# Batch 2's u centred by ScalarE, and the order around it: a fused attention, Fourier and two-layer kernel on one core

## The chip, the core and the metric

The kernel runs on one core of one Trainium2 chip. A core has five engines that run side by side, each through its own queue in order: TensorE (PE) for matmuls, VectorE (DVE), ScalarE (ACT) and GpSimd (POOL) for elementwise work, and SyncE (SP), which here issues nearly all DMAs. PE writes its results to PSUM; everything else is in SBUF or in DRAM. The metric is the time of one execution on the device in microseconds; the median of four runs before is 304.16 us (303.73 to 304.6).

## What is computed

Two blocks follow one another. Attention between x (8 batches, 8 heads, 512 rows, 64 columns) and a state of 32 rows gives 544 rows of 512 columns for each batch. The second block takes the real part of a two-dimensional Fourier transform of these rows, adds it, normalises and runs two layers with a residual.

```python
scores = scale * np.matmul(x, state.transpose(0, 1, 3, 2))      # softmax over the state rows
xread = np.matmul(softmax(scores), state)
scores2 = scale * np.matmul(state, x.transpose(0, 1, 3, 2))     # softmax over x's rows
sread = np.matmul(softmax(scores2), x)
x = np.concatenate([xread, sread], axis=2)                      # then (8, 544, 512)
mixed = np.real(np.fft.fft(np.fft.fft(x, axis=1), axis=2))
u = x + mixed
un = (u - mean(u)) / np.sqrt(var(u) + 1e-06)
out = u + np.maximum(un @ w_ch1, 0.0) @ w_ch2                   # 512 -> 2048 -> 512
```

The kernel computes the Exp of the scores without subtracting their maximum, and divides after the product. The division by the standard deviation (`rstd`) is put off to the very end, since it is positive and passes through the Relu: the layers work on u minus its mean, and the store multiplies by `rstd` and adds u.

## The kernel before

All engines run in the order in which the program text issues their instructions[...]. So the order of the calls is the schedule, and each call adds its instructions to the queues of several engines at once. A wait of the first instruction in a queue holds everything behind it.

A batch goes through these stages; the names are those of the code.

- `load_x`, `cast_x` bring x from DRAM as seven DMAs of SP, and POOL casts it to bf16 (`xin`).
- `attend(b)` gives two lists of steps. The first holds the scores: the transposes of x and state (`xT`, `sT`: by PE for batches 0 and 1, by SP's DMA transposes from batch 2 on, called `turned[b]`), then `scores` (x by state, Exp by ACT to `E`). The attention of x needs Exp of the scores the other way round, `ET`. Batch 1 computes it with matmuls of its own (`scores_t`, Exp again); from batch 2 on `turn_scores` turns `E` by matmuls with `ident` and `mirror`, and ACT's copy to `ET` also yields the sums over the rows. The second list R holds the reads: `read_low`, POOL's `fold_low` steps, `read(0)`, `sread_heads` or `sread_by_head`, `read(128)`, and `read(256)` with the folds. Each `xread` takes the one PSUM tile of pool psX, which DVE frees with its multiplication (L466).
- The folds add and subtract mirrored rows and columns (L529 to L549 on DVE, L514 to L526 on POOL), so that the Fourier matrices are a quarter of their size.
- `transform(b)` gives the steps T: four `over_s` (transform over rows, `G`), two `over_d` (over columns, `yp`), `add` (u, DVE), `centre` (statistics by DVE, u minus its mean to `ub`), `turn_u` (the transpose of `ub` to `unT`: by PE for batches 0 and 1, by a DMA transpose of SP (L852) from batch 2 on), `done`. u has four tiles of 128 rows, (0,1), (0,0), (1,1), (1,0) in this order. `flipped` names the batches whose `ub` ACT makes, with the sign turned.
- `layer1(b)` has 16 steps of four matmuls (0.86 us of PE each), each followed by a Relu of ACT to `hT`. For batch 0 they are quarter steps of sixteen small matmuls. A step takes a PSUM tile of pool psF, which has three.
- `layer2(b)` has 16 steps, four for a tile of u; the last of four stores: DVE multiplies and adds (L962, `ot`), SP issues the DMA. Of the first and the last tile the rows go through `r_dram`; the way back out of `r_dram` is issued just before the next store.

`first_roots` holds the computation of `rstd` (two POOL instructions, L343 and L344) for batches 0 and 1, which are called later than their statistics (`spread` for batch 0).

The opening (batches 0 and 1) is an order written out by hand. There L is `layer1(0)`, M is `layer2(0)`, s1 and r1 are the lists of `attend(1)`. Then a loop runs over b from 1 to 8. Pass 1 is by hand as well: M1 is what is left of `layer2(0)` (M1[0] is M[7]), L1 is `layer1(1)`, R and T belong to batch 2, s3 to batch 3. From pass 2 on `weave` merges the streams by position: each stream has a start and an end between 0 and 1, and its steps are spread evenly between. In pass 2 six steps of `layer2(1)` stand in the first 0.22, `layer1(2)` starts at 0.18, batch 3's reads run from 0.08 to 0.43, its T steps from 0.55 to 0.88. Worked out, pass 2 begins M M M R0 M R1 M R2 M and then the first step of `layer1(2)`, which needs all four tiles of `unT` of batch 2.

Three POOL copies to `gate` exist only to make POOL wait: for x's landing before the second half of w2 is loaded (L1162), for batch 1's folds before batch 2's x is cast (L1176), and for the last part of w2 before the last columns of it are cast (L1180). SP's transposes of x for batch 2 (`turned[2]`) wait for that last cast, and in SP's queue behind them stand `load_x(3)`, batch 0's first two stores, `turned[3]`, the state of the later batches, `load_x(4)`, the third store, and then the transposes of batch 2's `ub` with the fourth store after the first of them.

Of the kernel before, what the change touches and what calls it, by code (L numbers as in the profile page):

```python
# [15 lines left out]
AF = mybir.ActivationFunctionType  # L16
# [14 lines left out]
def kernel(  # L31
# [8 lines left out]
    nc = tc.nc  # L40
# [288 lines left out]
    def qt(name, dt=F32):  # L329
        return psQ.tile([128, 512 if dt == F32 else 1024], dt, name=name, tag="q")  # L330
# [29 lines left out]
    def attend(b):  # L360
# [52 lines left out]
        copies = []  # L413


        def scores_t(g):
            p = qt("eTp")
            for cols, rows in ((slice(0, 128), slice(0, 128)), (slice(128, 256), slice(255, 127, -1)),
                               (slice(256, 416), slice(256, 416)), (slice(416, 512), slice(511, 415, -1))):
                for hp in range(2):  # L420
                    nc.tensor.matmul(p[:, cols], lhsT=sT[:, 2 * g + hp, :], rhs=xT[:, 2 * g + hp, rows],
                                     start=(hp == 0), stop=(hp == 1))
            nc.scalar.activation(ET[:, g, :], p, AF.Exp, scale=scale)


        def scores(i):
            p = qt("esp")
            for si in (2 * i, 2 * i + 1):
                for pr in range(4):
                    hp = pr % 2  # L430
                    o = (si % 2) * 256 + pr * 64
                    nc.tensor.matmul(  # L432
                        p[:, o:o + 64].rearrange("p (h j) -> p h j", j=Ns),
                        lhsT=xT[:, pr, si * 128:(si + 1) * 128],
                        rhs=sT[:, pr, 64 * hp:64 * hp + 64].rearrange("p (h j) -> p h j", j=Ns)[:, :, ::-1 if b < 2 else 1],
                        start=True, stop=True)
            nc.scalar.activation(E[:, 2 * i:2 * i + 2].rearrange("p a b c -> p (a b c)"), p, AF.Exp, scale=scale)

# [48 lines left out]
        def sread_heads():  # L487
            p = qt("srp")
            for g in range(2):
                for si in range(4):  # L490
                    for hh in range(4):
                        c0 = 1 + 256 * g + 64 * hh
                        nc.tensor.matmul(p[32 * hh:32 * hh + 32, 64 * g:64 * g + 64], lhsT=E[:, si, g, 32 * hh:32 * hh + 32],
                                         rhs=xin[:, si, c0:c0 + 64], start=(si == 0), stop=(si == 3))
            for g in range(2):
                for si in range(4):
                    nc.tensor.matmul(p[:, 128 + g:129 + g], lhsT=E[:, si, g, :], rhs=xin[:, si, 0:1], start=(si == 0), stop=(si == 3))
            rcs = wk.tile([128, 2], F32, name="rcs", tag="rcs")
            nc.vector.reciprocal(rcs, p[:, 128:130])
            nc.vector.tensor_tensor(XQ[:, 0:2 * D].rearrange("p (g d) -> p g d", g=2),  # L500
                                    in0=p[:, 0:128].rearrange("p (g d) -> p g d", g=2),
                                    in1=rcs.unsqueeze(2).to_broadcast([128, 2, D]), op=ALU.mult)

        def state_rows():
            p = qt("hdp")
            pv = p[0:32, :].rearrange("p (h g d) -> p h g d", h=4, g=2)
            for hh in range(4):
                nc.tensor.matmul(pv[:, hh], lhsT=ident[:, 32 * hh:32 * hh + 32], rhs=XQ[:, 0:2 * D].rearrange("p (g d) -> p g d", g=2),
                                 start=True, stop=True)
            nc.scalar.copy(XR[0:32, 0, 512:0:-1].rearrange("p (g h d) -> p h g d", g=2, d=D), pv)  # L510

# [44 lines left out]
        if b < 2:  # L556
            first = [turn_state, lambda: turn_x(0), lambda: turn_x(1)]
            if b == 1:
                first = [turn_all] + [lambda i=i: copies[i]() for i in range(3)]
            first += [lambda: scores_t(0), lambda: scores_t(1),  # L560
                     lambda: scores(0), lambda: scores(1)]
        else:
            first = [lambda: scores(0), lambda: scores(1), lambda: turn_scores(1), lambda: turn_scores(0)]
            if b >= x_by_dma:
                turned[b] = lambda: (b > 2 and turn_state(), turn_x(0), turn_x(1))
                turned[b, 0] = turn_state
            else:
                first = [turn_state, lambda: turn_x(0), lambda: turn_x(1)] + first
# [129 lines left out]


    un_of, tiles_of = {}, {}  # L700
    flipped = (0, 1)

    def transform(b):
        g4, bq = b // 4, b % 4
# [154 lines left out]
        def done():  # L859
            tiles = []  # L860
            for k, r in order:
                if True:
                    u = U[k][:, r, 0:512] if r == 0 else U[k][:, r, 512:0:-1]
                    dst = {(0, 0): out[b, 1:129, :], (1, 1): out[b, 273:401, :], (0, 1): (b, 0, 543), (1, 0): (b, 1, 271)}[k, r]
                    tiles.append((u, rstds[k, r], dst))
            tiles_of[b] = tiles
            if b:
                keep_middle()
# [24 lines left out]
    def low_rows(g4):  # L893
# [15 lines left out]
        def turn_u():  # L909
            nc.sync.dma_start_transpose(out=unT, in_=m["ub"])  # L910
            dst = g4
            tiles_of[key] = [(m["U"], m["rstd"], dst)]

        return [over_d, centre, turn_u]

# [36 lines left out]
    def layer2(key):  # L952
# [2 lines left out]
        po_of = {}  # L955

        def store(i, cols):
            u, rstd, dst = tiles_of[key][i]
            while later:
                later.pop()()  # L960
            ot = wk.tile([128, dm], F32, name="ot", tag="ot", bufs=4)
# [168 lines left out]
    keep_low()  # L1130
    clears(1)
    clear_state(2, 3)
    state_blocks(2, 3, nc.gpsimd.tensor_copy)
    make_mirror()
    clear_state(3, 4)
    nc.gpsimd.tensor_tensor(gate, xs_of[0][:, 0:4], w1[:, :, 3 * 512], op=ALU.add)
    second_weights(0, 2)
# [2 lines left out]
    turned[2, 0]()  # L1140
    load_state(3, 4, s_dram)
    turn_u(0, 1)
    add_sums(0, 0)
    centre_sums(0, 0)
    copies1[0]()
    copies1[1]()
    warm(4)
    L[0]()
    s1[0]()
    copies1[2]()  # L1150
    L[1]()
    turn_u(0, 0)
    s1[1]()
    add_sums(1, 1)
    centre_sums(1, 1)
    add_sums(1, 0)
    L[2]()
    s1[2]()
    r1[0]()
    r1[1]()  # L1160
    r1[2]()
    nc.gpsimd.tensor_copy(gate, xs_of[2].rearrange("p (i c) -> p i c", i=4)[:, :, 0])  # L1162
    second_weights(2, 4)
    clear_state(4, B)
    L[3]()
    s1[3]()
    r1[3]()
    centre_sums(1, 0)
    L[4]()
    r1[4]()  # L1170
    r1[5]()
    turn_u(1, 1)
    L[5]()
    r1[6]()
    r1[7]()
    nc.gpsimd.tensor_copy(gate, XQs[1].rearrange("p (g j c) -> p g j c", g=2, j=4)[:, 1, 3, 0:4])  # L1176
# [5 lines left out]
    turned[2]()  # L1182
    load_x(3)
    turn_in_dram(4, B)
    L[6]()
    L[7]()
    turn_u(1, 0, nc.scalar.copy)
    spread(0, 1)
    state_ones(2, B)
    L[8]()  # L1190
    L[9]()
    L[10]()
    L[11]()
    over_s1(0)
    over_s1(1)
    L[12]()
    over_s1(2)
    over_s1(3)
    keep_middle()
    L[13]()  # L1200
    over_d1(0)
    add1(0, 1)
    L[14]()
    centre1(0, 1)
    over_d1(1)
    add1(0, 0)
    L[15]()
    centre1(0, 0)
    add1(1, 1)
    M[0]()  # L1210
    turn_u1(0, 1, nc.scalar.copy)
    M[4]()
    centre1(1, 1)
    add1(1, 0)
    M[1]()
    turn_u1(0, 0, nc.scalar.copy)
    centre1(1, 0)
    M[5]()
    M[2]()
    turn_u1(1, 1)  # L1220
# [74 lines left out]
```

## Time and profile before

| What | Value |
|---|---|
| median of four runs | 304.16 us |
| the profiled execution | 304.57 us |
| its span, first to last instruction | 302.8 us |
| DVE busy | 178.7 us (59%) |
| ACT busy | 136.6 us (45%) |
| POOL busy | 91.8 us (30%) |
| a step of layer 1 or 2 (four matmuls of 512 columns), start to start | 0.86 us |
| Relu of a step (ACT, L933) | 597 ns |
| `ub` by DVE (L847) / by ACT for batch 1 (L845) | 514 / 722 ns |
| statistics of a tile (DVE, L337 and L339) | 682 + 182 ns |
| `ot` of a store (DVE, L962) | 747 ns |
| `rstd` of a tile (POOL, L343 and L344) | 191 + 590 ns |

The page of a profile shows one execution: the busy time of each engine, the span in 40 slices (digits are tenths), the clock granted to PE, the chain of work that ended last, and groups of instructions by line. A line such as L962 is a line of the kernel. Besides the page the trace answers in time order (a timeline: start, length, engine, line, and in brackets how long the engine stood and who released it) and by stretches of time. The difference of 1.8 us between the profiled execution's time and its span lies before the first and after the last instruction.

### The profile page before, as it was taken

What the parts mean: (1) busy time and instruction counts of PE and PEld (TensorE: products, weight loads), DVE (VectorE), ACT (ScalarE), POOL (GpSimd) and SP (SyncE); (2) the same over time, 40 slices, a digit from 0 to 9 for tenths busy, and PEclk for the clock granted to TensorE, in tenths of its full rate; (3) what the DMA queues carried; (4) which work ended last, traced back from release to release, by engine and by line L of the source; (5) the groups of instructions that cost most, each with busy time, mean ns of one, the idle gap of its engine ahead of it and who ended that gap; (6) DMA issues with size and microseconds to landing.
All of it is one profiled execution on the core that took longest, in us unless ns stands there. A gap on an engine that the chain in (4) does not pass through costs nothing.

```text
span 302.8 us, 6030 instructions
## 1 busy us (share of the span) xinstructions
PE 288.0 (95%) x2302; PEld 164.9 (54%) x2333; DVE 178.7 (59%) x445; ACT 136.6 (45%) x254; POOL 91.8 (30%) x227
## 2 busy tenths in 40 slices
PE   5999998989969999999999999999999999999995
PEld 4789984545524545466544554455444544555443
DVE  8867987275938397664838485766668474000012
ACT  6888684535503553246533535244523442334200
POOL 6765944450391033500424022602240131000000
PEclk9999999999979999999999999999999999999999
DMA  8998993956863744566353784254333133500354
GB/s 155 193 204 184 169 148 70 190 114 141 172 142 79 164 114 71 122 140 157 48 129 73 158 154 89 71 122 87 81 80 69 37 85 82 130 6 29 95 129 125
DMA packets 110824, 34.86 MB, mean 115 GB/s; under 512 B 101980, under 2 KB 106332, under 8 KB 110796
## 3 DMA queue, kind: packets, MB, share of 16 engines
q1 hardware_dynamic: 100076, 28.72, 44.1%
q0 software_dynamic: 4224, 4.19, 9.5%
q10 hardware_dynamic: 6496, 1.57, 2.5%
q8 instruction: 18, 0.29, 0.4%
q14 instruction: 10, 0.08, 0.1%
HBM read 22.41 MB, written 14.02 MB: 120 GB/s over the span
## 4 chain that ended last, share of the span: by engine, by line
PE 85%; DVE 8%; issue 2%; ACT 2%; POOL 1%; DMA 1%; DVEq 0%; POOLq 0%
PE po L995 35%; PE ph L931 32%; PE ph L941 5%; PE gp L788 3%; PE yp L684 1%; PE yp L685 1%; PE po L987 1%; DVE ot L962 1%; PE xrp L457 1%; PE xfp L457 1%; PE esp L432 1%; DVE U L689 1%; DVE st L337 1%; PE eTp L444 1%; DMA unT<-ub 1%
## 5 line engine op out<-in xcount | busy, mean ns | idle before, releaser
L995 PE MATMUL po<-w,hT 128*128 128x512 bf16 x480 | 121.2, 379 | 2.2 <-ACT hT L933 0.9
L933 ACT ACTIVATE hT<-ph 128x512 bf16<-128x512 f32 x112 | 66.9, 597 | 123.9 <-PE ph L931 120.6
L931 PE MATMUL ph<-unT,w 128*128 128x512 bf16 x433 | 112.9, 381 | 3.4 <-DMA unT<-ub 2.4
L931 PEld LDWEIGHTS <-w 128*128 128x128 bf16 x576 | 50.6, 98 | 50.5 <-issue 4.5
L995 PEld LDWEIGHTS <-hT 128*128 128x128 bf16 x496 | 46.7, 98 | 47.8 <-issue 1.0
L962 DVE SCALAR_TENSOR_TENSOR ot<-po,rstd,U 128x512 f32<-128x512 f32 (+2 forms) x33 | 24.1, 731 | 50.6 <-PE po L995 48.4
L792 POOL COPY GL<-G 128x128 bf16<-128x128 bf16 x7 | 2.0, 291 | 73.9 <-ACT G L789 73.9
L337 DVE BATCH_NORM_STATS2 st<-U 128x6 f32<-128x512 f32 x32 | 21.8, 682 | 0.1
L689 DVE TENSOR_TENSOR U<-yp,XR 128x512 f32<-128x512 f32 x14 | 9.5, 682 | 20.1 <-PE yp L685 20.1
L344 POOL TENSOR_TENSOR rstd<-rstd,mhalf 128x1 f32<-128x1 f32 x34 | 20.1, 590 | 2.7
L343 POOL TENSOR_TENSOR rstd<-mv,epst 128x1 f32<-128x1 f32 x34 | 6.5, 191 | 45.3 <-DVE mv L339 45.3
L941 PE MATMUL ph<-unT,w 128*128 128x128 bf16 x256 | 16.2, 219 | 0.3 <-DVE unT L857 0.3
L941 PEld LDWEIGHTS <-w 128*128 128x128 bf16 x256 | 15.0, 98 | 0.5 <-issue 0.4
L789 ACT CAST G<-gp 128x288 bf16<-128x288 f32 x28 | 12.8, 483 | 4.4 <-PE gp L788 4.4
L847 DVE TENSOR_SCALAR ub<-U,mv 128x512 bf16<-128x512 f32 x24 | 12.3, 514 | 0.9
L148 POOL CAST xin<-xs 128x2048 bf16<-128x2048 f32 (+1 forms) x9 | 11.7, 1319 | 3.6 <-PE xfp L457 3.5
L943 ACT ACTIVATE hT<-ph 128x512 bf16<-128x512 f32 x16 | 9.5, 594 | 4.8 <-PE ph L941 4.7
L484 DVE TENSOR_TENSOR XR<-srp,rcs 32x128 bf16<-32x128 f32 x24 | 6.9, 287 | 6.4 <-PE srp L477 5.3
L514 POOL COPY XT<-XR 32x514 bf16<-32x514 bf16 x7 | 4.3, 608 | 19.9 <-DVE XR L466 19.9
L466 DVE TENSOR_TENSOR XR<-xrp,rs 128x512 bf16<-128x512 f32 x14 | 9.7, 695 | 0.5
L466 DVE TENSOR_TENSOR XF<-xfp,rs 128x512 bf16<-128x512 f32 x14 | 9.7, 692 | 0.5
L689 DVE TENSOR_TENSOR U<-yp,XF 128x510 f32<-128x510 f32 x14 | 9.4, 673 | 0.0
(245 smaller groups left out, 373.3 us busy)
## 6 DMA issues: line engine op xcount, KB each, us to landing
xs<-in_x_dram SPq DMA_DIRECT2D x22, 256.0 KB, 4.8
w<-in_moe_w_ch_dram POOLq DMA_DIRECT2D x8, 512.0 KB, 9.9
out_dram<-ot SPq DMA_DIRECT2D x15, 256.0 KB, 3.5
r_dram<-ot SPq DMA_DIRECT2D x14, 256.0 KB, 2.2
out_dram<-r_dram SPq DMA_DIRECT2D x14, 256.0 KB, 3.5
xs<-in_x_dram SPq DMA_DIRECT2D x8, 192.0 KB, 4.6
xs<-in_x_dram ACTq DMA_DIRECT2D x2, 256.0 KB
l_dram<-ot SPq DMA_DIRECT2D x2, 256.0 KB
```

Source lines behind the costliest of these rows:

```text
L148: copy(xin_bufs[b % 2][:, lo:hi, 1:513], xs_of[b].rearrange("p (i c) -> p i c", i=4)[:, lo:hi])
L337: nc.vector.bn_stats(st6, u)
L344: nc.gpsimd.tensor_tensor(rstd, rstd, mhalf, op=ALU.pow)
L466: nc.vector.tensor_tensor(ov, in0=p[ps, :, 0:256].rearrange("p g (h d) -> p g h d", d=D), in1=rs[ps].unsqueeze(3).to_broadcast([n, 2, 4, D ...
L689: nc.vector.tensor_add(u.rearrange("p (k r) -> p k r", r=2), p.rearrange("p (r k) -> p k r", r=2)[:, 0:u.shape[1] // 2, :], x.rearrange("p ...
L789: nc.scalar.copy(G[:, j, :].rearrange("p (i q) -> p q i", q=2), p[:, 0:NM].rearrange("p (q i) -> p q i", q=2))
L847: nc.vector.tensor_scalar(t, in0=ud, scalar1=mv[:, 0:1], scalar2=None, op0=ALU.subtract)
L931: nc.tensor.matmul(ph[:, o:o + n], lhsT=w1[:, c, f * 128:(f + 1) * 128], rhs=un_of[key][:, c, :], start=(c == 0), stop=(c == DC - 1))
L933: nc.scalar.activation(hT[:, per * i:per * i + per, :].rearrange("p a b -> p (a b)"), ph, AF.Relu, scale=-1.0 / 512 if key == 0 else -1.0 ...
L941: nc.tensor.matmul(ph[:, o:o + 128], lhsT=w1[:, c, f * 128:(f + 1) * 128], rhs=un_of[key][:, c, 128 * r:128 * r + 128], start=(c == 0), st ...
L962: nc.vector.scalar_tensor_tensor(ot[:, cols], in0=po_of[i][:, 0:cols.stop - cols.start], scalar=rstd, in1=u[:, cols], op0=ALU.mult, op1=AL ...
L995: nc.tensor.matmul(po_of[i], lhsT=h_of[key][:, f, i * 128:(i + 1) * 128], rhs=w2[:, f, :], start=(f == 0), stop=(f == FC - 1))
```

## The change

- Batch 1 loses `scores_t`. It now uses `scores` and `turn_scores` as the later batches do; its state is no longer taken in reverse order in `scores`, so `sread_heads` takes its sums from `turn_scores` and its rows are turned by `mirror` in `state_rows`. `make_mirror` goes ahead of `state_blocks(2, 3)` on POOL, the three copies of batch 1's transposes go ahead of `add_sums(0, 0)`, and the steps L and M stand two places further on against the reads and the T steps.
- `flipped` holds batch 2 too: ACT makes its four `ub`, and layer 1's Relu takes them with the sign turned.
- Of batch 0's statistics, `spread(1, 1)` and `spread(1, 0)` go behind the second store, with all roots but two. So that `done` can be called before, a tile holds a function that looks its `rstd` up.
- In pass 1, L1 starts later, `sread_by_head` (R[3]) goes ahead of `read(0)` (R[2]), the third store (M1[4]) goes between `read(0)` and `read(128)`, and M1[5], M1[6], M1[7] go further ahead of L1.
- In pass 2 seven steps of `layer2(1)` stand in the first 0.25, `layer1(2)` starts at 0.22, the reads at 0.1, the T steps at 0.57. Worked out: M M M R0 M R1 M M R2 M R3 and then `layer1(2)`; the load of x for batch 5 comes behind the store of batch 1's second tile, not ahead of it.

```diff
-        def scores_t(g):
-            p = qt("eTp")
...
-                    nc.tensor.matmul(p[:, cols], lhsT=sT[:, 2 * g + hp, :], rhs=xT[:, 2 * g + hp, rows],
-                                     start=(hp == 0), stop=(hp == 1))
-            nc.scalar.activation(ET[:, g, :], p, AF.Exp, scale=scale)
...
-                        rhs=sT[:, pr, 64 * hp:64 * hp + 64].rearrange("p (h j) -> p h j", j=Ns)[:, :, ::-1 if b < 2 else 1],
+                        rhs=sT[:, pr, 64 * hp:64 * hp + 64].rearrange("p (h j) -> p h j", j=Ns),
...
-            for g in range(2):
-                for si in range(4):
-                    nc.tensor.matmul(p[:, 128 + g:129 + g], lhsT=E[:, si, g, :], rhs=xin[:, si, 0:1], start=(si == 0), stop=(si == 3))
-            nc.vector.reciprocal(rcs, p[:, 128:130])
+            nc.vector.reciprocal(rcs, sums)
...
-                nc.tensor.matmul(pv[:, hh], lhsT=ident[:, 32 * hh:32 * hh + 32], rhs=XQ[:, 0:2 * D].rearrange("p (g d) -> p g d", g=2),
+                nc.tensor.matmul(pv[:, hh], lhsT=mirror[:, 96 - 32 * hh:128 - 32 * hh], rhs=XQ[:, 0:2 * D].rearrange("p (g d) -> p g d", g=2),
...
-            first += [lambda: scores_t(0), lambda: scores_t(1),
-                     lambda: scores(0), lambda: scores(1)]
+            first += [lambda: scores(0), lambda: scores(1), lambda: turn_scores(1), lambda: turn_scores(0)]
...
-    flipped = (0, 1)
+    flipped = (0, 1, 2)
...
-                    tiles.append((u, rstds[k, r], dst))
+                    tiles.append((u, lambda k=k, r=r: rstds[k, r], dst))
...
-            u, rstd, dst = tiles_of[key][i]
+            u, root, dst = tiles_of[key][i]
+            rstd = root()
...
+    make_mirror()
     state_blocks(2, 3, nc.gpsimd.tensor_copy)
-    make_mirror()
...
+    copies1[0]()
+    copies1[1]()
+    copies1[2]()
     add_sums(0, 0)
     centre_sums(0, 0)
-    copies1[0]()
-    copies1[1]()
     warm(4)
     L[0]()
     s1[0]()
-    copies1[2]()
+    s1[1]()
     L[1]()
     turn_u(0, 0)
-    s1[1]()
     add_sums(1, 1)
-    centre_sums(1, 1)
     add_sums(1, 0)
     L[2]()
     s1[2]()
+    s1[3]()
+    centre_sums(1, 1)
+    L[3]()
+    L[4]()
     r1[0]()
     r1[1]()
     r1[2]()
...
-    L[3]()
-    s1[3]()
+    L[5]()
+    r1[4]()
     r1[3]()
     centre_sums(1, 0)
-    L[4]()
-    r1[4]()
+    turn_u(1, 1)
+    L[6]()
     r1[5]()
-    turn_u(1, 1)
-    L[5]()
+    L[7]()
     r1[6]()
     r1[7]()
...
     turn_u1(1, 1)
-    M[6]()
+    done()
+    first_roots[0]()
+    M[3]()
+    spread(0, 0)
     turn_u1(1, 0)
-    spread(0, 0)
-    spread(1, 1)
-    spread(1, 0)
-    done()
-    for root in first_roots[0:1] + first_roots[5:8] + first_roots[1:5]:
-        root()
-    M[3]()
+    first_roots[5]()
     done1()
...
-        early, until, start = {2: (6, 0.22, 0.18), 3: (3, 0.13, 0.1)}.get(b, (0, 0, 0.08))
+        early, until, start = {2: (7, 0.25, 0.22), 3: (3, 0.13, 0.1)}.get(b, (0, 0, 0.08))
...
+            def spreads():
+                spread(1, 1)
+                spread(1, 0)
+                for root in first_roots[6:8] + first_roots[1:5]:
+                    root()
+
-            for step in (M1[0], L1[0], M1[1], s2[0], s2[1], M1[2], L1[1], s2[2], s2[3], lambda: cast_x(3), turned[3], M1[3], L1[2],
-                         lambda: load_state(4, B, s_dram), lambda: load_x(4), R[0], L1[3], R[1], R[2], L1[4], M1[4], R[3], L1[5], R[4],
-                         L1[6], R[6], L1[7], L1[8], M1[5], R[7], L1[9], M1[6], R[8], L1[10], L1[11], T[0], T[1], L1[12], T[2], T[3],
-                         M1[7], T[4], L1[13], T[5], s3[0], L1[14], T[6], s3[1], L1[15], T[7], M1[8], T[8], s3[2], s3[3], T[9], T[10],
+            for step in (M1[0], spreads, M1[1], M1[2], s2[0], s2[1], L1[0], M1[3], s2[2], s2[3], L1[1], lambda: cast_x(3), turned[3], L1[2],
+                         lambda: load_state(4, B, s_dram), lambda: load_x(4), R[0], L1[3], R[1], R[3], L1[4], R[2], L1[5], M1[4], R[4],
+                         L1[6], M1[5], R[6], L1[7], R[7], L1[8], M1[6], R[8], L1[9], L1[10], M1[7], T[0], T[1], L1[11], T[2], T[3],
+                         L1[12], T[4], L1[13], T[5], s3[0], L1[14], T[6], s3[1], L1[15], T[7], M1[8], T[8], s3[2], s3[3], T[9], T[10],
...
-            reads, mix = {2: ((0.08, 0.43), (0.55, 0.88)), 3: ((0.03, 0.4), (0.5, 0.86))}.get(b, ((0, 0.375), (0.47, 0.85)))
+            reads, mix = {2: ((0.1, 0.45), (0.57, 0.88)), 3: ((0.03, 0.4), (0.5, 0.86))}.get(b, ((0, 0.375), (0.47, 0.85)))
```

Between `turn_u(1, 0, nc.scalar.copy)` of batch 0 and `turn_u1(1, 1)`, which the diff above leaves out, the `over_s1`, `over_d1`, `add1`, `centre1` and `turn_u1` calls keep their order, and the L and M steps between them are those two places further on. Three steps of PE's work still stand between `over_d1(0)` and `turn_u1(0, 1)`; from `turn_u1(0, 0)` on it is one step fewer than before.

More of the change, by code (lines that the diff above doesn't have):

```diff
@@ L413, in attend @@
         copies = []
-        def scores_t(g):
-            p = qt("eTp")
-            for cols, rows in ((slice(0, 128), slice(0, 128)), (slice(128, 256), slice(255, 127, -1)),
-                               (slice(256, 416), slice(256, 416)), (slice(416, 512), slice(511, 415, -1))):
-                for hp in range(2):
-                    nc.tensor.matmul(p[:, cols], lhsT=sT[:, 2 * g + hp, :], rhs=xT[:, 2 * g + hp, rows],
-                                     start=(hp == 0), stop=(hp == 1))
-            nc.scalar.activation(ET[:, g, :], p, AF.Exp, scale=scale)
         def scores(i):
@@ L911, in turn_u @@
             dst = g4
-            tiles_of[key] = [(m["U"], m["rstd"], dst)]
+            tiles_of[key] = [(m["U"], lambda: m["rstd"], dst)]
         return [over_d, centre, turn_u]
@@ L1184 @@
     turn_in_dram(4, B)
-    L[6]()
-    L[7]()
+    L[8]()
+    L[9]()
     turn_u(1, 0, nc.scalar.copy)
@@ L1189 @@
     state_ones(2, B)
-    L[8]()
-    L[9]()
     L[10]()
     L[11]()
+    L[12]()
+    L[13]()
     over_s1(0)
     over_s1(1)
-    L[12]()
+    L[14]()
     over_s1(2)
@@ L1199 @@
     keep_middle()
-    L[13]()
+    L[15]()
     over_d1(0)
     add1(0, 1)
-    L[14]()
+    M[0]()
     centre1(0, 1)
@@ L1206 @@
     add1(0, 0)
-    L[15]()
+    M[4]()
     centre1(0, 0)
     add1(1, 1)
-    M[0]()
+    M[1]()
     turn_u1(0, 1, nc.scalar.copy)
-    M[4]()
     centre1(1, 1)
+    M[5]()
     add1(1, 0)
-    M[1]()
     turn_u1(0, 0, nc.scalar.copy)
     centre1(1, 0)
-    M[5]()
     M[2]()
+    M[6]()
     turn_u1(1, 1)
-    M[6]()
+    done()
+    first_roots[0]()
+    M[3]()
+    spread(0, 0)
     turn_u1(1, 0)
-    spread(0, 0)
-    spread(1, 1)
-    spread(1, 0)
-    done()
-    for root in first_roots[0:1] + first_roots[5:8] + first_roots[1:5]:
-        root()
-    M[3]()
+    first_roots[5]()
     done1()
```

## The prediction

> **What bounds the kernel now.** I read the page first: TensorE (PE) is busy 95% of a span of 302.8 us, and the chain that ended last is 85% PE. So a change can gain only where PE stands still, runs at a lower clock, or has work taken away. The page's row of PE clock shows one dent.
>
> ```profile
> PE   5999998989969999999999999999999999999995
> PEclk9999999999979999999999999999999999999999
> ```
>
> The busy time by stretches of about 3 us around the dent, and then the lines of PE's own timeline that end a wait (in brackets: its length and what ended it), give its size.
>
> ```profile
> 85.00:87.80 2.80, 0.44 (x3) 0.02 (x1) 0.69 (x2) 0.00 (x0) 2.62 (x6) 0.93 0.42 94
> 87.80:90.90 3.10, 2.96 (x38) 1.31 (x40) 0.55 (x2) 0.60 (x1) 3.10 (x6) 0.51 0.90 190
> ```
>
> ```profile
> 52.47 1.02 PE L995 MATMUL po<-w,hT 128*128 128x512 bf16 x4 [0.90 <-ACT hT L933]
> 64.53 0.40 PE L457 MATMUL xrp<-stb,ET 128*128 128x260 bf16 x2 [0.86 <-DVE XF L466]
> 84.19 0.40 PE L457 MATMUL xfp<-stb,ET 128*128 128x260 bf16 x2 [0.56 <-DVE XR L466]
> 87.81 1.87 PE L931 MATMUL ph<-unT,w 128*128 128x512 bf16 x4 [2.37 <-DMA unT<-ub]
> ```
>
> In the first fence PE's busy time is the figure after the length, the clock the third from the end. PE stands 2.37 us until the last transposed quarter of batch 2's u has landed; then the clock is 0.51 for some 3 us, and four matmuls take 1.87 us instead of 1.03. From 87.81 to 90.9 half the speed is lost: about 1.5 us. The three other waits are the largest before it.
>
> Who is late with unT? The critical chain blames VectorE (DVE). SyncE's (SP) timeline tells more:
>
> ```profile
> 47.00 5.12 SPq L388 DMA_TRANSPOSE xT<-xin  x4
> 52.17 5.36 SPq L145 DMA_DIRECT2D xs<-in_x_dram  x7
> 57.57 0.62 SPq L155 DMA_DIRECT2D s_dram<-in_state_dram  x1
> ...
> 78.38 0.38 SPq L966 DMA_DIRECT2D out_dram<-ot  x1
> 78.96 1.24 SPq L852 DMA_TRANSPOSE unT<-ub  x1
> 81.95 0.35 SPq L976 DMA_DIRECT2D r_dram<-ot  x1
> 82.76 3.83 SPq L852 DMA_TRANSPOSE unT<-ub  x3
> ```
>
> From 47.00 to 80.20 SP issues nearly without a break (one pause of 2.5 us for r_dram to land, at 59). The first transpose of u leaves at 78.96 though its ub was ready at 77.15. Then SP stands from 80.20 to 81.95 at the store of batch 0's last tile, which waits for DVE:
>
> ```profile
> 80.75 0.52 DVE L847 TENSOR_SCALAR ub<-U,mv 128x512 bf16<-128x512 f32 x1
> 81.19 0.73 DVE L962 SCALAR_TENSOR_TENSOR ot<-po,rstd,U 128x512 f32<-128x512 f32 x1
> ```
>
> Three transposes of about 1.25 us queue behind that store. So two queues in series, DVE and SP, set the dent.
>
> [...]waits of 0.9 us at 52 and 64 cost no clock.[...]
>
> **Opening (22 to 43 us).** Removed: `scores_t`, twice 0.45 us of PE (23.31 to 23.76, 24.88 to 25.32), and eight sum matmuls, 0.22 (29.59 to 29.81). Added: `turn_scores` twice, by batch 2's row 0.24 each. Net PE -0.63. On ACT two Exp of 0.60 become two Copy of 0.59 with a 0.2 accumulator read. What it gives back: add_sums(0,0) stands behind a DVE copy of 0.6 us and holds its PSUM tile until about 23.8, so the second Scores step may wait 0.3; read(128) and read(256) share one PSUM tile and now stand only one 0.89 step apart, with a DVE centring and copy (0.9) between: 0.5 together; the folds end about 1 us later, just when over_s1(2) wants them. From turn_u1(0,0) on batch 1's PE transposes come one step sooner, against ub of ACT that is ready 4.2 and 7.4 us after yp: about 0.3. Bounds: -0.6 to +1.0; I take +0.1, nearly nothing.
> POOL decides SP's start at 47.00: that waits for the cast behind the landing of w2's last part, issued about 35.6 and landed 46.5. Those loads stand behind `read_low`'s folds. I place XR for them near 29.6 (PE at 28.2 after L[4], then 1.2 us of DVE). POOL itself is free at 29.6, because the mirror (0.5 us) goes into its 4.07 us wait for a load. Before, the folds started at 30.08: I take the SP head 0.3 earlier, bounds 0.7 earlier to 1.0 later.
>
> **Statistics behind the stores (50 to 53).** Before, three statistics (2.4 us of DVE, 49.57 to 52.0) stand ahead of the first two stores, whose PSUM tiles PE wants. After, one stands between them, two follow. The 0.90 wait goes. Roots cost POOL 0.75 each and end about 56.6; the cast behind them starts only at 59.62, so that is covered.
>
> **Reads and store (57 to 66).** `sread_by_head` goes two steps ahead, the store between read 0 and read 128. DVE then has 1.2 (four 0.29) + 0.9 + 0.7 + 0.9 spread over five PE steps instead of standing in a row behind the store: the 0.86 wait and two of 0.17 and 0.10 go, 1.1 in all. Axes: L1[11] and M1[7] change places, both 0.86, so the T steps keep their place in PE's work and come 2.0 sooner only by these waits; the folds precede them by some 0.1 us for over_s(2), a margin I count as nothing.
>
> **Centring by ACT.** It removes four DVE instructions of 0.51 and adds four ACT ones; batch 1's row (L845) has 722 ns. But ACT is a queue: with yp at 0, mv(0,1) is there at 2.3 (74.3 to 76.6), then ub(0,1), Exp, the L1[14] Relu, ub(0,0), and the second Exp ends near 5.2. PE wants it for turn_scores at 4.2: a new wait of 1.05. Behind it ET comes near 8.6 against 8.3 wanted: 0.3. Bounds 0 to 2; 1.35 taken.
> DVE is relieved by 2.06 us, and all is 2.0 sooner: ot of the last tile comes near 78.2, not 81.9. SP then needs no wait: first transpose 78.96 as before, to 80.20; store at once, the next transpose 0.81 after it (as 81.95 to 82.76): 81.06; third starts 2.63 later (82.76 to 85.39): 83.69; PE follows 2.42 after (85.39 to 87.81): 86.1, less 0.3 for the head: **85.8**, 2.0 earlier.
>
> **Layer 1 of batch 2 later.** Seven layer-2 steps instead of six (0.86) and srp (0.36) stand ahead: 1.22 us of work moved ahead of the wait. Does PE get there in time? Before 85.45, less 0.90, 1.1, 0.56 and 0.1 of small ones, plus 1.22, 1.35 and the opening's 0.1: 85.5. So a gap of 0.3 is left, too short for the clock to fall. In batch 2's loop the next x load comes behind a store; SP's slack is 105.5 to 108.9 there, so I count nothing, up to +1 if the load delays batch 3.
>
> **Sum.** 2.0 (landing) + 1.2 (work done ahead) + 1.5 (clock) = 4.7. The waits at 52 and 64 aren't added: they are what lets PE arrive. The profiled execution took 304.57 (span 302.8); less 4.7: **299.8**. That run is at the upper of two values (303.7 and 304.6); the median of 304.16 is 0.4 lower. [...] I keep 299.8.
>
> **Rivals.**
> 1. Clock still halves (chance 0.14): SP's head isn't earlier and ACT's waits are at 2[...]: 299.8 + 1.5 + 0.4 = 301.7. [...] Against: 0.9 us gaps didn't do it.
> 2. Gain returned later (0.10): PE now runs 4.7 us ahead but SP only 2.4, and batch 3's u queues behind load_x(5): 1 to 2.5 us, 301.6. Against: SP's 3.4 us of slack.
> 3. Slower (0.08): the opening's new chain (Scores, Exp, turn, Copy, read) makes read_low late by d, hence POOL's folds, w2's landing, SP's head and unT. The price is d on the landing[...]. It decides from d = 3.2; with d = 4, 299.8 + 4 + 1.5 = 305.3. For: every link waits for the one before. Against: I find 0.5 us of slack, and a PSUM tile held by add_sums(1,0) would cost 1.4.
> 4. No change (0.05): moved waits reappear, 304.
>
> **Numbers.** Likeliest 0.63, 299.8, its own range 298.6 to 301: the waits of ACT and SP's head are its unknowns. 298.2 to 302.4 takes in rivals 1 and 2. Differences under 0.3% (0.9 us) can't be told from none. Faster: 0.63 + 0.14 + 0.10 = 0.87; same 0.05; slower 0.08.
>
> **What would show it.** Right: the first unT transpose for batch 2 still near 78.7, no break of SP behind it, PE clock 1.0 throughout; turn_scores waiting about 1 us for ACT; no waits at 52 and 64. Wrong: SP's transposes of xT starting after 48, or PE still over 1.5 us behind unT.

## The result, and the profile after

| What | Before | After |
|---|---|---|
| median | 304.85 us (64 runs) | 302.64 us (43 runs) |
| ratio, with its 95% interval | | 0.9945 [0.9932, 0.9959] |
| the profiled execution | 304.57 us | 305.21 us |
| the same kernel, profiled again in the first experiment | | 302.49 us |
| start of layer 1 of batch 2 | 87.81 us | 91.23 us; again: 88.51 us |
| from there to the end of the execution | 216.76 us | 213.98 us; again: 213.98 us |

The change makes the kernel faster by 2.2 us in the median, where 4.4 to 4.8 were predicted (299.8; the range ended at 298.2 and 302.4). The ratio lies near that of the means (304.74 and 303.01 us), which a few long executions raise; the ratio of the medians is 0.9927. Two executions each of runs 9 and 15 below are slow ones, over 1.5% above the fastest of the same kernel, and are left out of their medians and ratios. The execution that was profiled after the change is an unusual one: 36 of the 43 runs lie between 302.4 and 303.3, this one at 305.21. The other six long ones took 304.6 to 305.6; in four of them and in this one the mean granted clock is 0.993 or 0.994. So two profiles of the changed kernel are read below, this one and that of the first experiment.

The last two rows of the table are the key to all that follows. Everything after the start of layer 1 of batch 2 takes 213.98 us in both profiles of the changed kernel, 2.78 less than before: 1.22 of layer-2 and `srp` work moved ahead and some 1.5 of half clock, as predicted (run 8 below separates the two). Everything that went wrong happened before that start. It was to come at 85.8 and came at 88.5 and 91.2.

First the page's rows of PE and its clock in the profile after the change, and then its busy time by stretches (length, PE busy, PEld, DVE, ACT, POOL; the clock is third from the end).

```profile
PE   5998999869899999999999999999999999999995
PEclk9999999989999999999999999999999999999999
```

```profile
64.00:66.00 2.00, 0.17 (x1) 0.13 (x2) 1.91 (x6) 0.00 (x0) 2.00 (x6) 0.90 0.98 178
66.00:69.00 3.00, 3.00 (x9) 1.21 (x8) 1.33 (x3) 0.60 (x1) 0.65 (x2) 0.50 0.46 119
...
87.00:91.00 4.00, 4.00 (x35) 1.89 (x39) 2.43 (x6) 0.57 (x1) 3.77 (x9) 1.00 0.45 91
```

The dent at 87 is gone, with its half clock; a new one stands at 64 to 69, with its own. PE's timeline of the same profile names the waits:

```profile
54.85 0.41 PE L422 MATMUL esp<-sT,xT 128*128 128x64 bf16 x8 [1.05 <-DMA xT<-xin]
65.83 0.62 PE L447 MATMUL xfp<-stb,ET 128*128 128x260 bf16 x2 [2.29 <-DVE XF L456]
...
83.41 0.24 PE L434 MATMUL eTp<-ident,E 128*128 128x128 bf16 x2 [0.75 <-ACT E L427]
...
86.98 0.28 PE L447 MATMUL xrp<-stb,ET 128*128 128x260 bf16 x1 [0.29 <-ACT ET L435]
...
91.23 1.04 PE L917 MATMUL ph<-unT,w 128*128 128x512 bf16 x3
```

The 0.90 at 52 and the 0.86 of the reads are gone, the two waits for ACT are there with 0.75 and 0.29 us (1.05 and 0.3 were predicted), and layer 1 of batch 2 (L917) doesn't wait at all. But read 128 (`xfp`, L447) waits 2.29 us for DVE's XF of read 0: the two share one PSUM tile. DVE's timeline says why XF is late:

```profile
60.29 0.16 DVE L470 RECIPROCAL rcs<-sums 128x2 f32<-128x2 f32 x1
63.62 1.19 DVE L474 TENSOR_TENSOR XR<-srp,rcs 32x128 bf16<-32x128 f32 x4 [3.17 <-POOL XT L501]
65.08 0.69 DVE L456 TENSOR_TENSOR XF<-xfp,rs 128x512 bf16<-128x512 f32 x1
```

`sread_by_head` now stands ahead of read 0. Its four writes go into rows 0 to 31 of XR (L474), which POOL's copy `XT` (L501, part of `read_low`) must have read before. POOL's timeline, first of this profile:

```profile
54.82 0.19 POOL L343 TENSOR_TENSOR rstd<-mv,epst 128x1 f32<-128x1 f32 x1 [1.68 <-DVE mv L339]
...
59.03 0.55 POOL L344 TENSOR_TENSOR rstd<-rstd,mhalf 128x1 f32<-128x1 f32 x1
61.14 1.89 POOL L148 CAST xin<-xs 128x2048 bf16<-128x2048 f32 x1 [1.56 <-DMA xs<-in_x_dram]
62.98 0.61 POOL L501 COPY XT<-XR 32x514 bf16<-32x514 bf16 x1
```

The copy stands behind `cast_x(3)` (L148), the cast behind six roots and, here, behind the landing of batch 3's x. In the kernel before the same instructions stood like this on POOL and DVE:

```profile
55.55 0.55 POOL L344 TENSOR_TENSOR rstd<-rstd,mhalf 128x1 f32<-128x1 f32 x1
59.62 1.89 POOL L148 CAST xin<-xs 128x2048 bf16<-128x2048 f32 x1 [3.52 <-PE xfp L457]
61.46 0.61 POOL L514 COPY XT<-XR 32x514 bf16<-32x514 bf16 x1
...
62.32 1.19 DVE L484 TENSOR_TENSOR XR<-srp,rcs 32x128 bf16<-32x128 f32 x4
```

There the last root ended at 56.10, the copy at 62.07, and the writes came just behind it without a wait. (The trace names a matmul of read 0 as what ended the cast's wait; the program issues that one after the cast, so it can't be. The landing of x fits: in five other profiles in which the cast waits for x, it starts 12.5 to 12.7 us after SP's head, that is the start of SP's transposes of xT; here 12.6.) SP's timeline explains the landing:

```profile
48.45 5.12 SPq L388 DMA_TRANSPOSE xT<-xin  x4
53.62 5.26 SPq L145 DMA_DIRECT2D xs<-in_x_dram  x7
...
79.16 0.38 SPq L953 DMA_DIRECT2D out_dram<-ot  x1
81.31 1.22 SPq L838 DMA_TRANSPOSE unT<-ub  x1
84.17 0.36 SPq L963 DMA_DIRECT2D r_dram<-ot  x1
85.06 3.83 SPq L838 DMA_TRANSPOSE unT<-ub  x3
```

SP's head is at 48.45 here, 1.45 later than before, and in the usual run at 46.16. A late head makes Scores wait for xT (1.05 at 54.85), x late, and XT late. So this execution has the usual loss of read 128 (1.9, below) in a longer form (2.29), a half clock after it, and 1.05 on top.

### The profile page after: what moved, and what is told of

Its sections match the earlier page's. It is cut to its first block, busy times and chain, and to the rows that moved or that the text cites. A ratio compares the mean times of both kernels' runs of the same rounds, so it can differ in the third digit from the quotient of the medians.

```text
span 303.4 us, 6004 instructions
## 1 busy us (share of the span) xinstructions
PE 288.0 (95%) x2288; PEld 164.0 (54%) x2319; DVE 176.5 (58%) x441; ACT 139.4 (46%) x260; POOL 90.7 (30%) x227
## 4 chain that ended last, share of the span: by engine, by line
PE 70%; DMA 12%; SPq 7%; DVE 6%; POOL 2%; issue 2%; ACT 1%; ACTq 0%; POOLq 0%; DVEq 0%
PE po L982 31%; PE ph L917 30%; DMA s_dram<-in_state_dram 7%; SPq L145 5%; DMA xs<-in_x_dram 3%; PE gp L774 2%; DMA gen<-s_dram 2%; SPq L388 1%; PE po L974 1%; PE yp L671 1%; PE yp L670 1%; DVE U L675 1%; DVE st L337 1%; PE xfp L447 1%; PE xrp L447 1%
## 5 line engine op out<-in xcount | busy, mean ns | idle before, releaser
L917 PE MATMUL ph<-unT,w 128*128 128x512 bf16 x432 | 112.6, 381 | 0.9 <-DVE ot L949 0.3
L917 PEld LDWEIGHTS <-w 128*128 128x128 bf16 x576 | 50.5, 98 | 46.4 <-issue 1.5
L343 POOL TENSOR_TENSOR rstd<-mv,epst 128x1 f32<-128x1 f32 x34 | 6.5, 191 | 45.1 <-DVE mv L339 45.1
L148 POOL CAST xin<-xs 128x2048 bf16<-128x2048 f32 (+1 forms) x9 | 11.7, 1319 | 1.6 <-DMA xs<-in_x_dram 1.6
L455 DVE RECIPROCAL rs<-xrp 128x8 f32<-128x8 f32 x14 | 2.9, 206 | 14.6 <-PE xrp L447 14.6
L427 ACT ACTIVATE E<-esp 128x512 bf16<-128x512 f32 x14 | 8.3, 596 | 5.2 <-PE esp L422 5.2
L833 DVE TENSOR_SCALAR ub<-U,mv 128x512 bf16<-128x512 f32 x20 | 10.3, 514 | 0.7
L501 POOL COPY XT<-XR 32x514 bf16<-32x514 bf16 x7 | 4.3, 609 | 19.9 <-DVE XR L456 19.8
```

What stands on the lines that cost most here:

```text
L148: copy(xin_bufs[b % 2][:, lo:hi, 1:513], xs_of[b].rearrange("p (i c) -> p i c", i=4)[:, lo:hi])
L917: nc.tensor.matmul(ph[:, o:o + n], lhsT=w1[:, c, f * 128:(f + 1) * 128], rhs=un_of[key][:, c, :], start=(c == 0), stop=(c == DC - 1))
```

## The experiments

In each group of runs the kernel before ran beside them, with medians of 304.62 to 304.68. "Start" is the start of layer 1 of batch 2 in the profile.

| Run | Median, us | Ratio to before | Start, us |
|---|---|---|---|
| 1 changed, again | 302.52 | 0.9943 [0.9920, 0.9965] | 88.51 |
| 2 cast behind `read_low` | 300.76 | 0.9885 [0.9852, 0.9917] | 87.85 |
| 3 read order undone | 301.23 | 0.9896 [0.9865, 0.9927] | 87.19 |
| 4 centring by DVE | 303.18 | 0.9980 [0.9958, 1.0003] | 89.32 |
| 5 run 2, state's cast last | 300.74 | 0.9861 [0.9839, 0.9882] | 86.80 |
| 6 run 2, opening mended | 300.07 | 0.9844 [0.9814, 0.9874] | 86.32 |
| 7 both | 299.60 | 0.9833 [0.9804, 0.9863] | 85.80 |
| 8 run 2, layer 1 not later | 301.51 | 0.9888 [0.9862, 0.9914] | 85.75 |
| 9 before, new read order | 305.18 | 1.0023 [1.0002, 1.0043] | 86.88 |
| 10 before, cast behind `read_low` | 304.57 | 0.9986 [0.9966, 1.0006] | 87.72 |
| 11 run 7, one centring by DVE | 300.18 | 0.9861 [0.9833, 0.9889] | 86.26 |
| 12 run 7, statistics undone | 300.25 | 0.9866 [0.9840, 0.9892] | 86.13 |
| 13 changed, roots behind reads | 300.53 | 0.9866 [0.9842, 0.9889] | 86.56 |
| 14 changed, state's cast last | 302.69 | 0.9944 [0.9928, 0.9960] | 88.52 |
| 15 changed, both of these | 300.76 | 0.9893 [0.9868, 0.9918] | 86.87 |
| 16 changed, roots and opening mended | 302.28 | 0.9929 [0.9904, 0.9955] | 88.34 |

### 1 to 4: where the loss sits

Three theories: A, the reads (XT late on POOL); B, the queue of ScalarE; C, the opening. The changed kernel again:

> The changed kernel itself, for a profile of a usual execution: the profiled one took 305.21 us where the median is 302.64. All theories: 302.4 to 302.9. Theory A (the gain was lost in batch 2's reads: sread_by_head's writes on VectorE wait for GpSimd's copy XT, which stands behind cast_x(3) and so behind x's landing): TensorE waits 1.5 to 2.3 us at read(128) (xfp) in every profile, also with the clock at 1.0. Theory B (ScalarE's queue took it): the waits at turn_scores and at the first read behind it sum to over 2 us. Theory C (the opening took it): yp of batch 1 comes at 42.4 or later and no wait above 1 us follows before 70.

PE's timeline of this run, and POOL's:

```profile
64.66 0.40 PE L447 MATMUL xfp<-stb,ET 128*128 128x260 bf16 x2 [1.89 <-DVE XF L456]
80.69 0.25 PE L434 MATMUL eTp<-ident,E 128*128 128x128 bf16 x2 [0.75 <-ACT E L427]
84.26 0.28 PE L447 MATMUL xrp<-stb,ET 128*128 128x260 bf16 x1 [0.29 <-ACT ET L435]
...
88.51 1.04 PE L917 MATMUL ph<-unT,w 128*128 128x512 bf16 x4
```

```profile
55.28 0.19 POOL L343 TENSOR_TENSOR rstd<-mv,epst 128x1 f32<-128x1 f32 x1 [1.69 <-DVE mv L339]
...
59.48 0.55 POOL L344 TENSOR_TENSOR rstd<-rstd,mhalf 128x1 f32<-128x1 f32 x1
59.98 1.89 POOL L148 CAST xin<-xs 128x2048 bf16<-128x2048 f32 x1
61.81 0.60 POOL L501 COPY XT<-XR 32x514 bf16<-32x514 bf16 x1
```

In the usual run the cast starts at 59.98 with no idle time ahead of it: it isn't x that it waits for but the six roots.

```diff
-  L1[1], lambda: cast_x(3), turned[3], L1[2],
-  lambda: load_state(4, B, s_dram), lambda: load_x(4), R[0], L1[3], R[1], R[3],
+  L1[1], L1[2], R[0], lambda: cast_x(3), turned[3],
+  lambda: load_state(4, B, s_dram), lambda: load_x(4), L1[3], R[1], R[3],
```

> cast_x(3), turned[3] and the two loads behind them go one layer-1 step and R[0] later, so that GpSimd copies XT before it waits for x of batch 3; SyncE's and TensorE's order stay. Theory A: the wait of 2.3 us at xfp goes to under 0.3, the kernel is 1.2 to 2 us faster than the changed one (about 301.0). Theories B and C: no difference (within 0.3 us).

PE's timeline of run 2 at read 128:

```profile
63.66 0.39 PE L447 MATMUL xfp<-stb,ET 128*128 128x260 bf16 x2
```

The wait of read 128 goes, and with it 1.76 us of the median (302.52 to 300.76). The profile is of a run above the median (301.8): SP's head came at 48.74, Scores waited 0.84 for xT and layer 1 0.29 for unT, hence the start of 87.85.

```diff
-  R[1], R[3], L1[4], R[2], L1[5], M1[4], R[4],
+  R[1], R[2], L1[4], R[3], L1[5], M1[4], R[4],
```

> R[2] (read 0) goes ahead of R[3] (sread_by_head) again, everything else as changed. Theory A: VectorE's XF of read 0 no longer stands behind the writes that wait for XT; the wait at xfp shrinks by about 1 us: 301.3 to 301.8. Theories B and C: 302.5, no difference.

It goes here too; waits of 0.17 and 0.25 are left in the reads. So the wait needs both the new order and the late XT.

```diff
-    flipped = (0, 1, 2)
+    flipped = (0, 1)
```

> flipped is (0, 1) again: VectorE makes batch 2's ub. Theory B: the waits for ScalarE at turn_scores (0.75) and the first read (0.29) go and the kernel gets 0.7 to 1.1 us faster, 301.6. Theories A and C: no gain; VectorE has 2 us more to do ahead of the last store and unT, so layer 1 of batch 2 waits up to 1 us: 302.5 to 303.5.

PE's timeline of the fourth run:

```profile
89.32 1.02 PE L917 MATMUL ph<-unT,w 128*128 128x512 bf16 x4 [1.90 <-DMA unT<-ub]
```

The two waits for ACT (1.04) go, and 1.90 for unT comes. So centring by ACT is worth 0.66 in the median, and B isn't the loss.

### 5 to 8: what else was missed

Run 5 moves `state_blocks(3, 4)`, POOL's four casts of batch 3's state, behind the last cast of batch 2's x:

```diff
-    state_blocks(3, 4, nc.gpsimd.tensor_copy)
     nc.gpsimd.tensor_copy(gate, w2[:, 12:16, 0])
     cast_columns(508, 512, slice(0, 4))
+    state_blocks(3, 4, nc.gpsimd.tensor_copy)
```

> Second experiment's kernel (casts behind read_low), and with it POOL's four casts of batch 3's state set behind the last cast of batch 2's x, so that SP's transposes of xT no longer hang on the state's way through DRAM. Theory D (that way sets SP's head, and its length differs from run to run: the head was 45.8 to 48.9 in five profiles): the head starts at 45.5 or sooner in every profile, no wait of Scores for xT, unT's last quarter 0.5 to 2 us sooner, the wait of layer 1 of batch 2 (0.29) gone; 300.0 to 300.6 and no run above 301.2. Rival E (w2's landing sets the head): head stays at 46 to 47, time stays at 300.8 within 0.3.

SP's head came at 45.1, but the median didn't move. Theory D is of no weight for the median; whether it explains the rare long runs is taken up with run 14.

```diff
     L[0]()
-    s1[0]()
-    s1[1]()
     L[1]()
+    s1[0]()
+    L[2]()
+    s1[1]()
     turn_u(0, 0)
...
-    L[2]()
+    L[3]()
     s1[2]()
     s1[3]()
```

The layer-1 steps behind these move up by one likewise, until L[8], and `turn_u(1, 1)` goes ahead of `centre_sums(1, 0)`.

> Second experiment's kernel, and with it the opening's scores one layer-1 step later each, so that the first no longer meets DVE's copy of xT nor the second add_sums' PSUM tile (0.49 and 0.45 in the changed kernel); the turn of u(1,1) goes ahead of a centring. Theory C (the opening lost 0.44 more than was predicted, by these two waits): both go, layer 2 of batch 0 starts 0.4 to 0.9 sooner, 300.0 to 300.4. Rival (the waits come back at the reads or at over_s1): 300.8 within 0.3.

Both waits of the opening go: 0.69 us of the median, though the six runs spread from 299.32 to 301.98. Then run 7, with the edits of 5 and 6:

> Both edits of the two kernels before. If they are independent their gains add: 299.3 to 300.0, the prediction's own number. If one covers the other, the better of the two.

PE's timeline of run 7, all waits over 0.2 us from 23 us to layer 1 of batch 2:

```profile
77.97 0.24 PE L434 MATMUL eTp<-ident,E 128*128 128x128 bf16 x2 [0.75 <-ACT E L427]
...
81.55 0.28 PE L447 MATMUL xrp<-stb,ET 128*128 128x260 bf16 x1 [0.29 <-ACT ET L435]
...
85.80 1.04 PE L917 MATMUL ph<-unT,w 128*128 128x512 bf16 x4
```

The fastest kernel of the study: 299.60, 5.0 less than the kernel before beside it. Start and time are those of the prediction (85.8 and 299.8), the start in part by luck: 85.8 was predicted as the landing of unT, with PE there 0.3 sooner; here PE comes at 85.80 and waits for nothing. Run 8 sets batch 2's pacing back in run 2's kernel (`early` 6 in place of 7, the old points for reads and transform):

> Second experiment's kernel with batch 2's pacing as before the change (six layer-2 steps ahead instead of seven, reads and transform at the old points). Prediction's term (1.22 us of work stands ahead of the wait): layer 1 of batch 2 reaches its wait 1.2 sooner and waits about 1.5 for unT, the clock stays at 1.0: 301.8 to 302.2. Rival (unT isn't last there any more, the term is empty): 300.8 within 0.3.

The start comes 1.05 sooner than in run 5's profile (85.75 against 86.80) and the rest takes 215.26 in place of 214.03: the moved work is 1.23, as predicted. No wait for unT shows in this profile, which is of a run below the median (301.01); the median is 0.75 worse than run 2's, less than the 1.2 of the theory. Moving work ahead of a wait is worth only the wait that it fills, and in this profile none was left.

### 9 and 10: the same edits in the kernel before

Run 9 takes the new order of the reads into the kernel before; read 0 and the third store come one layer-1 step later with it:

```diff
-  R[1], R[2], L1[4], M1[4], R[3], L1[5], R[4],
+  R[1], R[3], L1[4], R[2], M1[4], L1[5], R[4],
```

> The kernel before, with one thing of the change alone: batch 2's sread_by_head goes ahead of read 0. Theory A (its writes into XR wait on DVE for POOL's copy XT, which stands behind cast_x(3)): a wait of 1 to 2.5 us of a read for DVE's XF near 62 to 65; slower by 1 to 2 us, 305.6 to 306.6. Rival (the loss belongs to the order of all parts together): 304.6 within 0.5.

> The kernel before, with cast_x(3) and what goes with it behind read_low, as in the second experiment. Theory A (there is no wait of sread_by_head's writes in the kernel before, so the place of the cast is worth nothing by itself): 304.6 within 0.5. Rival (the late cast is a gain of its own, which the second experiment only put on top): faster by 1 us or more.

Run 10 came as theory A said: no gain by itself. Run 9, at 305.18, came between the two expectations. DVE's timeline, and PE's, in run 9:

```profile
59.85 1.19 DVE L484 TENSOR_TENSOR XR<-srp,rcs 32x128 bf16<-32x128 f32 x4 [0.87 <-POOL XT L514]
```

```profile
63.57 0.40 PE L457 MATMUL xrp<-stb,ET 128*128 128x260 bf16 x2 [0.24 <-DVE XF L466]
...
86.88 1.02 PE L931 MATMUL ph<-unT,w 128*128 128x512 bf16 x4 [2.40 <-DMA unT<-ub]
```

In this profile XT is early enough: the roots end near 55.9, the cast starts at 57.38 upon x's landing. The 0.86 wait of the reads falls to 0.24, nearly as the prediction had it, and the old wait for unT swallows the gain. So the order of the reads doesn't make the wait where XT comes early. But the profile is of one of the shortest runs (303.84), with SP's head at 44.88; with the 47.00 of the profile before, where XT ended at 62.07, it would by estimate end about 3 us after the 58.98 at which the writes could have begun here. The kernel was 0.6 slower than before in the median, with an interval just clear of 1; whether its longer runs have this wait isn't known, as none was profiled. What makes XT late, the roots or the landing, was left open.

### 11 and 12: the centring and the statistics, in the best kernel

> Seventh experiment's kernel (casts behind read_low, state's cast last, opening mended), and the second of batch 2's four centrings, which stands on ACT ahead of the Exp that turn_scores waits for, by DVE instead. Theory B in its remaining size (ACT's queue costs 0.75 + 0.29 at turn_scores): the 0.75 falls to 0.15 or less, 298.9 to 299.2. Rival (DVE 0.5 later makes unT's last quarters late, layer 1 of batch 2 waits): 299.6 within 0.3.

PE's timeline and ACT's of run 11:

```profile
81.27 0.28 PE L447 MATMUL xrp<-stb,ET 128*128 128x260 bf16 x1 [1.06 <-ACT ET L435]
```

```profile
79.92 0.72 ACT L831 ACTIVATE ub<-U,mv 128x512 bf16<-128x512 f32 x1 [0.73 <-DVE mv L339]
80.54 0.58 ACT L435 ACTIVATE ET<-eTp 128x512 bf16<-128x512 f32 x1
```

A miss for both theories: the 0.75 goes at `turn_scores` and comes back as 1.06 at the read behind it, because the copy to ET queues on ACT behind the last centring, which waits for DVE's statistics. The median is 0.58 worse.

> Seventh experiment's kernel, with the statistics and roots of batch 0 ahead of the first stores, as before the change. Prediction's step (a wait of 0.90 at layer 2 near 52 goes): 300.2 to 300.6. Rival (half of it comes back as waits for the turned u of batch 1, as the traces of the change show): 299.6 to 300.0.

Worth 0.65 in the median. A wait of 0.89 comes back, at 49.85, where PE's transpose waits for a centred u of batch 1 (`ub`, by ACT), rather than at the store.

### 13 to 16: roots or landing

```diff
-    for root in first_roots[6:8] + first_roots[1:5]:
+    for root in first_roots[6:8]:
         root()
...
-  R[2], L1[5], M1[4], R[4],
+  R[2], L1[5], M1[4], R[4], *first_roots[1:5],
```

> The changed kernel, with the four roots of batch 1 (3.1 us of POOL, not wanted before 78) behind batch 2's reads. Theory F (roots alone make XT late): cast_x(3) starts at 57, XT ends at 59.5, the 1.89 wait goes: 300.6 to 300.9. Theory G (both: the landing of x is next, near 59): cast starts at 58.5 to 59.2, the wait falls to 0.8 to 1.2: 301.3 to 301.9. Theory H (the landing alone): 302.5 within 0.2.

POOL's timeline of run 13, then PE's:

```profile
57.95 1.89 POOL L148 CAST xin<-xs 128x2048 bf16<-128x2048 f32 x1 [0.94 <-DMA xs<-in_x_dram]
59.78 0.61 POOL L501 COPY XT<-XR 32x514 bf16<-32x514 bf16 x1
```

```profile
86.56 1.04 PE L917 MATMUL ph<-unT,w 128*128 128x512 bf16 x3
```

With four roots gone from ahead of it the cast starts 2.0 sooner, XT follows, the 1.89 wait is gone, and the median falls by 2.1 to 300.53 (from 302.64). This is just under theory F's range, with the landing next in line. SP's head was at 45.41 here, 0.75 sooner than in run 1, so not all of the 2.0 is the roots': with a head at 46.16, x would have landed near 58.8 (an estimate from the 12.5 to 12.7 us above), and about 0.7 of the wait would have been left.

> The changed kernel, with POOL's state casts behind batch 2's last cast, so that SP's head comes near 45.2. Theories F and G (the roots still end at 60.0): the 1.89 wait stays, 302.5 within 0.2, and no run above 303.5. Theory H: cast starts a microsecond sooner, 301.3 to 301.7.

Nothing, as F and G said for the median. But three of 22 runs lie at 304.5 to 305.1 (mean clock 0.992 or 0.993, where the others have 0.998 or more) although SP's head no longer hangs on the state: what was expected of the long runs failed. Both edits together:

> Both edits of the two runs before. Theory G: XT ends by 60.6, the wait is 0 to 0.3, 300.6 to 300.9. Theory F: as the first of the three. Theory H: as the second.

The profile has SP's head at 45.63, the cast at 58.33 after 1.45 of waiting for x, and a wait of 0.27: between F and G. Five of all its 16 runs took 302.7 or more. The last run mends the roots and the opening, and leaves the cast where the change has it:

> The changed kernel with only two things mended: batch 1's four roots behind batch 2's reads (alone 300.53) and the opening's scores one layer-1 step later (0.7 in the sixth run). Theory: these two are all that the prediction missed, the gains add: 299.6 to 300.0. Rival (they cover each other, as the unT landing is next): 300.2 to 300.5, with layer 1 of batch 2 waiting for unT.

POOL's timeline and PE's in run 16:

```profile
59.81 1.89 POOL L148 CAST xin<-xs 128x2048 bf16<-128x2048 f32 x1 [3.67 <-DMA xs<-in_x_dram]
```

```profile
64.49 0.40 PE L447 MATMUL xfp<-stb,ET 128*128 128x260 bf16 x2 [2.32 <-DVE XF L456]
```

Neither expectation: the wait is back, at 2.32. SP's head is at 47.10 here (45.41 in run 13), so x lands 1.9 later, while PE, with a better opening, comes sooner. POOL's timeline shows what the head waited for: in run 16 the state of batch 3 (1.96 ahead of its cast), in run 7 the last part of w2 (3.34 ahead of `gate`). Of the five profiles with the mended opening, four have the head at 46.5 to 47.3 (runs 6, 7, 11, 16) and one at 44.85 (run 12), so it isn't shown that the mended opening makes it late. All six of run 16's executions are longer than run 13's, and that stays unexplained. So theory G in the end: XT has two things ahead of it on POOL, the roots and the landing, and with the roots out of the way the landing decides. Moving the cast itself behind XT (runs 2, 5 to 8, 11 and 12) is the mend that holds with heads between 44.9 and 48.7.

## Why the prediction was wrong

The direction and the mechanism at unT were right; the arrival of PE at layer 1 of batch 2 was not.

- **The step that failed** is in "Statistics behind the stores": "Roots cost POOL 0.75 each and end about 56.6; the cast behind them starts only at 59.62, so that is covered." The statistics, moved behind the second store, were done only at 55.2 to 56.0; six roots of 0.79 us start at 55.3 and end at 60.0, where the last one ended at 56.10 before. The 59.62 was no fixed start either: it was x's landing with SP's head at 47.0. With a head at 45.4 the cast can start at 57.95 (run 13). So in run 1 cast and XT are some 2 us later than in run 13.
- **"Reads and store"** took the waits of 0.86, 0.17 and 0.10 as gone, and they went. But the step counted DVE's durations in the new order and not what the moved instruction waits for: `sread_by_head` writes what XT reads. In the old order its writes started at 62.32, just after XT's end at 62.07, and never waited; moved ahead of read 0 they hold DVE's queue, and PE waits 1.89. The wait goes if the old order comes back (run 3), if the cast goes behind XT (run 2) or if four roots go (run 13). The term is worth 1.76 in the median of run 2; in run 13, whose head was earlier too, the start comes 1.95 sooner.
- **Opening**: +0.1 was taken, within bounds of -0.6 to +1.0. Its waits are 0.49 for DVE's copy of xT and 0.45 for the PSUM tile of `add_sums` (0.5 in all was counted for two waits) and 0.40 at the reads. Mending gives 0.69 (run 6 against 2) and 1.14 (run 7 against 5). A mis-sized term, of some 0.7 us: start 86.56 in run 13 against 85.8.
- These two make the difference: by the starts of runs 1, 13 and 7, 1.95 and 0.76 are the 2.7 between the usual 302.49 and 299.8. Run 16 mends just these two, but x's landing came in between; so that they alone make the whole loss isn't shown by one run.
- **SP's head**, taken 0.3 earlier with bounds of 0.7 earlier to 1.0 later: in run 1 0.84 earlier, in the profile after 1.45 later. It was put down to the landing of w2's last part; in both these profiles POOL waits for the state of batch 3 instead (0.83 and 3.55 us). Over all profiles it lies between 44.6 and 48.7.
- **Centring by ACT**: waits of 1.05 and 0.3 were predicted, 0.75 and 0.29 measured. Right; undoing it costs 0.66 (run 4).
- **Layer 1 later (1.22) and the clock (1.5)**: right in size. The rest of the execution takes 213.93 to 214.03 in all fourteen profiles with both, 215.26 with the work not moved (run 8), 216.76 before: 1.2 to 1.3 for the work and 1.50 for the clock.
- **unT's landing at 85.8**: the first transpose in run 1's profile left at 78.59 (predicted 78.7), but SP then stood until 81.45 for the store, because DVE was 2 us late. In run 7 the store comes at 79.67 and PE doesn't wait at 85.80. So of the signs named for being right, the first transpose near 78.7 and the clock of 1.0 came true in run 1; SP without a break and no wait at 64 did not.
- **Rival 1** (the clock still halves) was the fate of the execution profiled after the change, from another wait than it named. Rival 3's chain, from the opening's reads to a late unT, can't be the loss, since layer 1 doesn't wait for unT.

What stays open: SP's head and the few long runs. POOL's timelines show what the head follows: the landing of the state in the profile after and in runs 1, 6 and 16 (waits of 3.55, 0.83, 2.36 and 1.96), that of w2's last part in the profile before and, with the state's cast out of the way, in runs 5 and 7 (1.83, 1.00 and 3.34); why the same two transfers take so different times isn't shown. The state's way alone doesn't explain the long runs (run 14).

## What to carry to other kernels

When a step is moved forward, look at what each of its instructions must wait for on other engines, also those that only have to have read what it writes; an order that has never waited may simply have come after by chance. A queue "covered" by a wait is covered only as long as that wait's own end stays; write down what sets it. Where a kernel has one place through which everything passes, split the time there: the part behind it was the same to 0.1 us in fourteen profiles, and each loss could be read off the part ahead.

## What the runs showed of the hardware

- After a wait of PE of about 2.3 us the clock was half in some profiles and full in another. In the kernel before, 2.37 us was followed by 0.51 for some 3 us; in the changed kernel's first profile 2.29 us was followed by 0.50 for about 3 us. In run 16, 2.32 us at almost the same place left it full: the four matmuls of the layer-1 step just behind (64.72) take 1.03 us, where the four behind the 2.37 take 1.87, and the mean clock of that execution is 1.0. Waits of 1.89 to 1.91 left the mean at 1.0 in the profiles of runs 1, 4 and 14. What decides between the two isn't shown. The two values of the kernel before go with the clock: of its 136 executions beside the experiments, 32 with a mean clock of 0.999 or 1.0 took 302.9 to 303.9, 104 with 0.989 to 0.994 took 304.2 to 306.9. Run 10, whose profile has the clock at 0.50 from 88 to 90, shows the same two groups: 7 of its 22 executions at 0.999 or 1.0 took 302.9 to 303.8, 15 at 0.994 took 304.3 to 305.7.
- The state's way from DRAM to DRAM (64 KB) took, from its issue to the issue of the load that waits for it, 7.0 us in the profile before (28.82 to 35.82) and 10.7 in the one after (29.92 to 40.63): one and the same transfer.
